# A weight product moved to the front of TensorE, with the first attention batch placed by hand inside it

## The chip, the cores and the metric

One core of one Trainium2 chip. The metric is the device time of one execution in microseconds (us), median of several executions; the profile's "span" of an execution is 1.7 to 2.3 us shorter in the runs of this case. Where a granted clock is given, it is the mean over an execution or a stretch of the clock that the profile says TensorE was granted (1.000 is full). "Half clock" below names a pace, read from the distance of matmuls of 512 columns: 0.42 to 0.43 us where the fastest stretches have 0.216 (kernel before, from 26.38 and from 29.74 us), or from other work that takes longer in such stretches (score groups 0.66 us instead of 0.43). The granted clock doesn't show every one of them (it reads 1.00 in that one); that the clock is the cause there is the author's reading.

## The reference

```python
scores = q @ k.T / 8                      # 8 batches, 8 heads, 576 positions, 64 channels
# heads 0-3 see the last 32 positions; heads 4-7 every 4th of the last 128
attn = softmax(where(mask, scores, -1e9))
x = (attn @ v) -> [4608, 512]             # heads side by side
a, b = x @ w1, x @ w2                     # 512 -> 1024
y = ((a * b) @ w3) @ w_out                # 1024 -> 1024 -> 512
```

Both kernels form `wf = w3 @ w_out` once on the chip, so that y is `(a * b) @ wf`: 64 matmuls in place of a whole layer.

## The kernel before

Four kinds of work share TensorE. The attention of a batch is four *steps* (dilated heads `d0`, `d1`, plain heads `p0`, `p1`), each of two score groups (12 small matmuls, exponential on ScalarE, mask on VectorE), values (12 matmuls, then reciprocal and scaling on VectorE) and a transpose to channels (6 matmuls and a copy into `XT`). `ffn1(t, f)` makes an eighth of a and b for block `t` (512 tokens) in 8 matmuls of 512 columns, and VectorE multiplies a by b. `ffn2(t, tb)` makes 128 rows of y in 8. The weight product has `fuse_t` (8 transposes of w3 and a copy to `w3T`) and `fuse_m` (8 matmuls and a copy to `wf`).

The attention is a list of *phases*. `point()` stands before each group of four large matmuls, and a table of marks (point number, phases done by then) says how many phases to place there:

```python
def fuse_t(ft):
    xv = ps_x.rearrange("p (g x) -> p g x", g=KFF)      # the bank that to_channels uses too
    for g in range(KFF):
        nc.tensor.transpose(out=xv[:, g, :], in_=w3n[ft // 2][...], identity=ident)
    w3T[ft] = wk_pool.tile([P, KFF, P], BF16, tag="w3T", bufs=2, name="w3T")
    nc.scalar.copy(out=w3T[ft], in_=xv)
...
load_qk(0, split=True); load_vp(0); load_w12(0, 512); load_qk(1); load_vd(1); load_vp(1)
load_w12(512, 1024); load_wo()
for g in range(4): load_w3(g)
for ph in phases[:n0]: ph()                  # batch 0, all its 22 phases
marks = [(0, n0), (9, n0), (30, done_at[7]), (32, done_at[7]), (54, done_at[11]), ...]
for f in range(KFF): ffn1(0, f, point)
fuse_t(0)
for ft in range(KFF):
    if ft + 1 < KFF: fuse_t(ft + 1)
    fuse_m(ft, point)
for f in range(KFF): ffn1(1, f, point)
for tb in range(4): ffn2(0, tb, point)
for t in range(2, NT): ...                   # two ffn1 of t, one ffn2 of t - 1, in turn
```

`done_at[7]` is the last phase of batch 1, `done_at[11]` of batch 2. Block 1 needs all of batch 1, block 2 all of batch 2, and so on.

The softmax here doesn't subtract the row's maximum and nothing guards it: scores larger than these inputs give would overflow.

Of the kernel before, what the change touches and what calls it, by code (L numbers as in the profile page):

```python
# [35 lines left out]
def kernel(  # L36
# [29 lines left out]
    stage = ExitStack()  # L66
    ps_early = stage.enter_context(tc.tile_pool(name="pse", bufs=1, space=bass.MemoryType.PSUM))
# [21 lines left out]
    ps_e = ps_early.tile([P, 2, TB], F32, name="ps_e")  # L89
    ffn_psum = []  # L90

    def bank():
        if not ffn_psum:
            ffn_psum.append(
                ctx.enter_context(
                    tc.tile_pool(name="psf", bufs=3, space=bass.MemoryType.PSUM)
                )
            )
        return ffn_psum[0].tile([P, TB], F32, tag="f", name="f")
# [4 lines left out]
    def load_qk(b, split=False):  # L104
        for nm, dst, src in (("qn", qn, q), ("kn", kn, k)):
            dst[b] = qk_pool.tile([P, 2, ROWS * D], BF16, tag=nm, name=nm)
        for u in (1, 0) if split else (slice(0, 2),):
            if split and u == 0:
                const_pool()
                load_vd(b)  # L110
            for dst, src in ((qn, q), (kn, k)):
                x = src[b].rearrange("(u h) (j a) d -> (h j) u (a d)", u=2, a=ROWS)
                nc.gpsimd.dma_start(out=dst[b][:, u], in_=x[:, u])  # L113
# [46 lines left out]
    def load_wo():  # L160
        nc.gpsimd.dma_start(out=wo_sb, in_=moe_w_out.rearrange("(a p) f -> p a f", p=P))
# [77 lines left out]
    class Step:  # L239
# [5 lines left out]
        def scores(self, hp, sp):  # L245
            u, hf = self.u, self.hf
            qt, kt = qts[u][self.b % 2], kts[u][self.b % 2]
            for m in range(3 * hf, 3 * hf + 3):
                for c in range(2):
                    for g in range(2):  # L250
                        prt = slice(32 * (2 * hp + g), 32 * (2 * hp + g) + 32)
                        if u:
                            rhs = qt[prt, 96 * m : 96 * m + 96, c]
                        else:
                            rhs = qt[prt].rearrange("p (s i) c -> p s i c", s=4)
                            rhs = rhs[:, :, 24 * m : 24 * m + 24, c]
                        c0 = 96 * (m - 3 * hf)
                        nc.tensor.matmul(  # L258
                            out=sp[:, g, c0 : c0 + 96],
                            lhsT=kt[prt, 96 * m : 96 * m + P, c],  # L260
                            rhs=rhs,
                            start=(c == 0),
                            stop=(c == 1),
                        )
# [3 lines left out]
            nc.scalar.activation(out=ev, in_=sp[:, :, 0:HALF], func=ACT.Exp, scale=scale)  # L268
# [62 lines left out]
    early = [True]  # L331
# [16 lines left out]
    def s_tile(hp):  # L348
        return ps_e if early[0] and hp else ps_s

    def later(f, *args):
        phases.append(lambda: f(*args))

    def segment(lo, hi):

        for i in range(lo, hi + 2):
# [5 lines left out]
            if i == lo:  # L362
                later(transpose_qk, b, 1, 0)
                later(transpose_qk, b, 1, 1)
                if lo:
                    later(spread_vd, b)
            if at == 2 and more:
                later(transpose_qk, b + 1, 1, 0)
            if at == 3 and more:
                later(transpose_qk, b + 1, 1, 1)  # L370
            if st is not None:
                later(lambda st=st: st.scores(0, s_tile(0)))
# [5 lines left out]
            if st is not None:  # L378
                later(lambda st=st: st.scores(1, s_tile(1)))
                if at == 0:  # L380
                    later(transpose_qk, b, 0, 0)
                    if b == 0:
                        later(spread_vd, 0)
                if at == 1:
                    later(transpose_qk, b, 0, 1)
                    later(prefetch, b + 2)
                if at == 3 and more:
                    later(spread_vd, b + 1)

    segment(0, 4)  # L390
# [42 lines left out]
    def ffn2(t, tb, point):  # L433
# [12 lines left out]
        o_sb = wk_pool.tile([P, d_model], F32, tag="osb", bufs=3, name="osb")  # L446
# [5 lines left out]
    def fuse_t(ft):  # L452
        xv = ps_x.rearrange("p (g x) -> p g x", g=KFF)
# [6 lines left out]
        w3T[ft] = wk_pool.tile([P, KFF, P], BF16, tag="w3T", bufs=2, name="w3T")  # L460
        nc.scalar.copy(out=w3T[ft], in_=xv)  # L461

    def fuse_m(ft, point):
        point()
        ps = bank()
        for g in range(KFF):
            if g == KFF // 2:
                point()
            nc.tensor.matmul(  # L469
                out=ps,  # L470
# [5 lines left out]
        nc.vector.tensor_copy(out=wf_sb[:, ft, :], in_=ps)  # L476
# [3 lines left out]
    load_qk(0, split=True)  # L480
    load_vp(0)
    load_w12(0, 512)
# [3 lines left out]
    load_w12(512, 1024)  # L486
    load_wo()
    for g in range(4):
        load_w3(g)

    const_spread()
    n0 = done_at[3]
    for ph in phases[:n0]:
        ph()
    early[0] = False
    stage.close()
# [4 lines left out]
        (0, n0), (9, n0), (30, done_at[7]), (32, done_at[7]), (54, done_at[11]),  # L501
    ]
    for t in range(3, 8):
        marks.append((54 + 24 * (t - 2), done_at[4 * t + 3]))
    xs, ys = [m[0] for m in marks], [m[1] for m in marks]
    state = [0, n0]
# [7 lines left out]

    for f in range(KFF):
        ffn1(0, f, point)
    fuse_t(0)
    for ft in range(KFF):
        if ft + 1 < KFF:
            fuse_t(ft + 1)  # L520
        fuse_m(ft, point)
    for f in range(KFF):
        ffn1(1, f, point)
    for tb in range(4):
        ffn2(0, tb, point)
    for t in range(2, NT):
# [37 lines left out]
```

## Time and profile before

| | before |
|---|---|
| time, median of 4 | 289.98 us (289.5 to 290.55) |
| first scores | 9.13 us |
| first a, b matmul | 26.38 us |
| first w3 transpose | 45.14 us |
| product of a and b for block 3, first of eight | 131.67 us |
| granted clock | 1.000 in the profiled run |

The rows are starting times in the trace. From block 3 on both kernels issue the same order of a, b and y, so the fourth row is where a gain or loss of the change must already be complete. The prediction shows the page and the busy time by stretches; the second and fourth row are these lines (start, duration, engine, line, operation; in brackets the idle time before and what ended it):

```profile
26.38 9.62 PE L406 MATMUL f<-XT,w_sb 128*128 128x512 bf16 x36 [0.73 <-ACT XT L327]
...
131.67 0.69 DVE L417 TENSOR_TENSOR gt<-f,asb 128x512 bf16<-128x512 f32 x1 [0.45 <-PE f L406]
```

### The profile page before, as it was taken

How to read it: one execution, taken by the hardware profiler on the slowest of the kernel's cores; microseconds unless marked ns; L12 is line 12 of the kernel's file. 1: busy time of each engine (PE TensorE's matmuls, PEld its weight loads, DVE VectorE, ACT ScalarE, POOL GpSimd, SP SyncE). 2: the span in 40 equal slices, each digit the busy share in tenths (PEclk: the TensorE clock that was granted, in tenths of full speed). 3: DMA queues.
4: the chain of work that ended last, by engine and by line, in shares of the span. 5: the costliest groups of instructions: out<-in, count | busy, mean ns of one | idle time of the engine just before them, and what ended most of it. 6: DMA issues, size and time to landing. Idle time of an engine off the chain costs nothing.

```text
span 288.0 us, 5662 instructions
## 1 busy us (share of the span) xinstructions
PE 260.3 (90%) x2336; PEld 131.8 (46%) x2336; DVE 164.8 (57%) x356; ACT 123.8 (43%) x200; POOL 53.7 (19%) x77
## 2 busy tenths in 40 slices
PE   0466988879899999999999999999999999999994
PEld 0353435444345545444444445445545544444441
DVE  5573385545798776767677767776764443222110
ACT  1543245543446455444544454455444433332422
POOL 8943512350042042006000600000000000000000
PEclk9999999999999999999999999999999999999999
DMA  7999999999069289567907991111111121111133
GB/s 102 156 207 190 198 211 210 202 194 144 0 102 171 75 166 173 80 116 130 137 36 124 145 147 42 39 36 39 39 36 39 36 56 55 36 73 36 48 85 126
DMA packets 50746, 30.51 MB, mean 106 GB/s; under 512 B 37920, under 2 KB 40992, under 8 KB 50720
## 3 DMA queue, kind: packets, MB, share of 16 engines
q0 software_dynamic: 45088, 20.71, 57.5%
q1 hardware_dynamic: 5632, 9.44, 10.9%
q8 instruction: 18, 0.29, 0.4%
q14 instruction: 8, 0.07, 0.1%
HBM read 41.41 MB, written 9.44 MB: 177 GB/s over the span
## 4 chain that ended last, share of the span: by engine, by line
PE 82%; DMA 9%; POOL 3%; ACT 2%; DVE 2%; issue 1%; POOLq 0%; ACTq 0%
PE f L406 41%; PE f L439 22%; PE ps_s L258 7%; DMA qn<-in_q_dram 5%; DMA w_sb<-in_moe_w_dram 4%; PE f L469 4%; PE ps_o L287 4%; PE ps_x L312 3%; PE ps_x L455 1%; ACT w3T L461 1%; POOL vst L137 1%; POOL vp L128 1%; POOL w_sb L155 1%; ACT et L268 0%; POOL qn L113 0%
## 5 line engine op out<-in xcount | busy, mean ns | idle before, releaser
L406 PE MATMUL f<-XT,w_sb 128*128 128x512 bf16 x576 | 138.8, 383 | 2.0 <-DMA w_sb<-in_moe_w_dram 1.3
L417 DVE TENSOR_TENSOR gt<-f,asb 128x512 bf16<-128x512 f32 x72 | 49.5, 687 | 55.5 <-PE f L406 55.3
L406 PEld LDWEIGHTS <-w_sb 128*128 128x128 bf16 x576 | 52.5, 98 | 61.1 <-issue 3.1
L439 PE MATMUL f<-wf_sb,gt 128*128 128x512 bf16 x288 | 70.8, 379 | 0.0
L416 ACT CAST asb<-f 128x512 bf16<-128x512 f32 x72 | 42.2, 586 | 54.3 <-PE f L406 49.6
L268 ACT ACTIVATE et<-ps_s 128x576 bf16<-128x576 f32 x60 | 39.2, 653 | 40.1 <-PE ps_s L258 39.9
L447 ACT COPY osb<-f 128x512 f32<-128x512 f32 x36 | 21.1, 586 | 45.7 <-PE f L439 45.7
L258 PE MATMUL ps_s<-qt,kt 32*128 32x96 bf16 x720 | 26.9, 206 | 13.8 <-DVE kt L230 10.1
L439 PEld LDWEIGHTS <-gt 128*128 128x128 bf16 x288 | 25.2, 98 | 25.2
L258 PEld LDWEIGHTS <-kt 32*128 32x128 bf16 x768 | 19.3, 97 | 37.0 <-issue 20.2
L297 DVE TENSOR_TENSOR xo<-ps_o,rcp 96x768 bf16<-96x768 f32 x32 | 30.5, 953 | 1.1
L137 POOL DMA_DIRECT2D vst<-in_v_dram x32 | 21.3, 672 | 13.9 <-DMA w3n<-in_moe_w_dram 4.4
L270 DVE TENSOR_TENSOR et<-et,mask_pl 128x576 bf16<-128x576 bf16 x32 | 14.6, 457 | 15.8 <-ACT et L268 15.5
L270 DVE TENSOR_TENSOR et<-et,mask_di 128x576 bf16<-128x576 bf16 x32 | 14.6, 456 | 14.7 <-ACT et L268 14.5
L230 DVE STREAM_TRANSPOSE qt<-qn 128x160 uint32<-128x160 uint32 (+1 forms) x64 | 19.6, 421 | 1.9 <-DMA qn<-in_q_dram 1.9
L287 PEld LDWEIGHTS <-et 128*128 128x128 bf16 x384 | 17.0, 102 | 7.7 <-issue 1.2
L312 PE MATMUL ps_x<-ident,xo 96*128 96x96 bf16 x192 | 14.4, 215 | 5.4 <-ACT w3T L461 2.3
L312 PEld LDWEIGHTS <-xo 96*128 96x128 bf16 x192 | 11.9, 102 | 12.5 <-DVE xo L297 4.1
L113 POOL DMA_DIRECT2D qn<-in_q_dram x9 | 6.3, 696 | 61.1 <-DVE qt L230 57.9
L296 DVE RECIPROCAL rcp<-ps_o 96x12 f32<-96x12 f32 x32 | 7.2, 225 | 16.4 <-PE ps_o L287 16.3
L469 PE MATMUL f<-wo_sb,w3T 128*128 128x512 bf16 x64 | 16.0, 380 | 0.0
L327 ACT COPY XT<-ps_x 128x576 bf16<-128x576 bf16 x18 | 11.5, 640 | 7.7 <-PE ps_x L312 7.7
(43 smaller groups left out, 113.8 us busy)
## 6 DMA issues: line engine op xcount, KB each, us to landing
qn<-in_q_dram POOLq DMA_DIRECT2D x7, 576.0 KB, 8.7
kn<-in_k_dram POOLq DMA_DIRECT2D x7, 576.0 KB, 7.8
vp<-in_v_dram POOLq DMA_DIRECT2D x7, 384.0 KB, 9.8
w_sb<-in_moe_w_dram POOLq DMA_DIRECT2D x4, 512.0 KB, 11.9
w3n<-in_moe_w_dram POOLq DMA_DIRECT2D x4, 512.0 KB, 18.7
out_dram<-osb SPq DMA_DIRECT2D x8, 256.0 KB, 2.3
out_dram<-osb SPq DMA_DIRECT2D x8, 224.0 KB, 2.3
out_dram<-osb SPq DMA_DIRECT2D x8, 192.0 KB, 2.2
```

Source lines behind the costliest of these rows:

```text
L137: nc.gpsimd.dma_start(out=vsts[b % 2][p0 : p0 + n, m, :, :], in_=bass.AP(tensor=x.tensor, offset=x.offset + (4 * i0 + 2 * second) * D, ap= ...
L258: nc.tensor.matmul(out=sp[:, g, c0 : c0 + 96], lhsT=kt[prt, 96 * m : 96 * m + P, c], rhs=rhs, start=(c == 0), stop=(c == 1),)
L268: nc.scalar.activation(out=ev, in_=sp[:, :, 0:HALF], func=ACT.Exp, scale=scale)
L270: nc.vector.tensor_tensor(out=ev, in0=ev, in1=mk.unsqueeze(1).to_broadcast([P, 2, HALF]), op=AL.mult)
L287: nc.tensor.matmul(out=ps_o[:, hp, j * (D + 1) : (j + 1) * (D + 1)], lhsT=self.et[:, c0 : c0 + P], rhs=rhs, start=True, stop=True,)
L297: nc.vector.tensor_tensor(out=xo[0:96], in0=ov[:, :, :, 0:D], in1=rcp[0:96].unsqueeze(3).to_broadcast([96, 2, 6, D]), op=AL.mult,)
L312: nc.tensor.transpose(out=xo, in_=self.xo[0:96, hp, 2 * m : 2 * m + 2, :], identity=ident[0:96, 0:96],)
L406: nc.tensor.matmul(out=ps, lhsT=w_sb[:, c, f * P : (f + 1) * P], rhs=XT[:, c, t0 + lo : t0 + hi], start=(c == 0), stop=(c == DCH - 1),)
L416: nc.scalar.copy(out=a_sb[:, 0 : hi - lo], in_=ps)
L417: nc.vector.tensor_tensor(out=gts[t][:, f, lo:hi], in0=pss[1], in1=a_sb[:, 0 : hi - lo], op=AL.mult)
L439: nc.tensor.matmul(out=y, lhsT=gts[t][:, f, tb * P : (tb + 1) * P], rhs=wf_sb[:, f, :], start=(f == 0), stop=(f == KFF - 1),)
L469: nc.tensor.matmul(out=ps, lhsT=w3T[ft][:, g, :], rhs=wo_sb[:, g, :], start=(g == 0), stop=(g == KFF - 1),)
```

## The change

The intent: TensorE's front is thin because it waits for the chain of attention steps of batch 0 (busy 9.4 of the first 26.3 us). The weight product doesn't depend on attention, so it could fill those waits. w3 and w_out are loaded first; the order in the front is written out by hand ("T": `fuse_t`, "M": half a `fuse_m`, "A": one attention phase); the w3T transposes leave the attention's bank and are copied by ScalarE and VectorE in turn; the second score buffer of the early stage goes; y of blocks 0 and 1 comes right behind their a and b, so that 24 points still pass before batch 1 must be done (its phases stand in the last 11 of them).

```diff
+    ps_f = ctx.enter_context(tc.tile_pool(name="psf", bufs=3, space=bass.MemoryType.PSUM))
-    ps_e = ps_early.tile([P, 2, TB], F32, name="ps_e")
...
-        xv = ps_x.rearrange("p (g x) -> p g x", g=KFF)
+        xv = bank().bitcast(BF16).rearrange("p (g x) -> p g x", g=KFF)
...
-        nc.scalar.copy(out=w3T[ft], in_=xv)
+        (nc.vector.tensor_copy if ft % 2 else nc.scalar.copy)(out=w3T[ft], in_=xv)
...
-    load_qk(0, split=True)
+    load_w3(0); load_wo(0); load_wo(1); const_pool(); load_w3(1); load_qk(0, 1)
+    load_w3(2); load_vd(0); load_qk(0, 0); load_w3(3)
     load_vp(0)
-    load_w12(0, 512)
+    load_w12(0, 256); load_w12(256, 1024)
...
+    for what in (
+        "T0 T1 M0 M0 M1 M1 T2 T3 M2 M2 M3 A M3 A T4 T5 M4 A M4 A M5 A M5 A "
+        "T6 T7 M6 A M6 A A M7 A A M7 A A A A A"
+    ).split(): ...
...
-        (0, n0), (9, n0), (30, done_at[7]), (32, done_at[7]), (54, done_at[11]),
+        (0, done_at[3]), (13, done_at[3]), (24, done_at[7]), (27, done_at[7]),
+        (47, done_at[11]), (53, done_at[11]), (64, done_at[15]),
...
+    for t in range(2):
+        for f in range(KFF): ffn1(t, f, point)
+        for tb in range(4): ffn2(t, tb, point)
     for f in range(KFF):
-        ffn1(0, f, point)
-    fuse_t(0)
-    ...
-    for t in range(2, NT):
+        ffn1(2, f, point)
+    for t in range(3, NT):
```

The 16 phases of batch 0 are, in order: four score groups of d0 and d1, values d0, values d1, channels d0, channels d1, four score groups of p0 and p1, values p0, values p1, channels p0, channels p1. Transposes of q and k and the copy of v (`spread_vd`) ride along with the phase that first needs them. In the kernel before they were phases of their own (hence 22 for batch 0), and the steps of batch 0 overlapped: the next step's scores stood before a step's values. Not shown in the cut: `w3T` gets three buffers in place of two and the tile of y six in place of three.

More of the change, by code (lines that the diff above doesn't have):

```diff
@@ L65 @@
     psum = ctx.enter_context(tc.tile_pool(name="ps", bufs=1, space=bass.MemoryType.PSUM))
-    stage = ExitStack()
-    ps_early = stage.enter_context(tc.tile_pool(name="pse", bufs=1, space=bass.MemoryType.PSUM))
+    ps_f = ctx.enter_context(tc.tile_pool(name="psf", bufs=3, space=bass.MemoryType.PSUM))
     w1_sb = const.tile([P, DCH, d_ff], BF16, name="w1_sb")
@@ L88, with load_qk @@
     ps_x = psum.tile([P, 2 * TB], BF16, name="ps_x")
-    ps_e = ps_early.tile([P, 2, TB], F32, name="ps_e")
-    ffn_psum = []
     def bank():
-        if not ffn_psum:
-            ffn_psum.append(
-                ctx.enter_context(
-                    tc.tile_pool(name="psf", bufs=3, space=bass.MemoryType.PSUM)
-                )
-            )
-        return ffn_psum[0].tile([P, TB], F32, tag="f", name="f")
+        return ps_f.tile([P, TB], F32, tag="f", name="f")
     qn, kn = {}, {}
-    def load_qk(b, split=False):
+    def load_qk(b, us=slice(0, 2)):
         for nm, dst, src in (("qn", qn, q), ("kn", kn, k)):
-            dst[b] = qk_pool.tile([P, 2, ROWS * D], BF16, tag=nm, name=nm)
-        for u in (1, 0) if split else (slice(0, 2),):
-            if split and u == 0:
-                const_pool()
-                load_vd(b)
-            for dst, src in ((qn, q), (kn, k)):
-                x = src[b].rearrange("(u h) (j a) d -> (h j) u (a d)", u=2, a=ROWS)
-                nc.gpsimd.dma_start(out=dst[b][:, u], in_=x[:, u])
+            if b not in dst:
+                dst[b] = qk_pool.tile([P, 2, ROWS * D], BF16, tag=nm, name=nm)
+            x = src[b].rearrange("(u h) (j a) d -> (h j) u (a d)", u=2, a=ROWS)
+            nc.gpsimd.dma_start(out=dst[b][:, us], in_=x[:, us])
     def load_vp(b):
@@ L158, in load_w12, with load_wo @@
             )
-    def load_wo():
-        nc.gpsimd.dma_start(out=wo_sb, in_=moe_w_out.rearrange("(a p) f -> p a f", p=P))
+    def load_wo(half):
+        a = slice(4 * half, 4 * half + 4)
+        nc.gpsimd.dma_start(
+            out=wo_sb[:, a, :], in_=moe_w_out.rearrange("(a p) f -> p a f", p=P)[:, a, :]
+        )
     w3n = {}
@@ L243, in __init__, with scores @@
             self.xo = {}
-        def scores(self, hp, sp):
+        def scores(self, hp):
             u, hf = self.u, self.hf
@@ L258, in scores @@
                         nc.tensor.matmul(
-                            out=sp[:, g, c0 : c0 + 96],
+                            out=ps_s[:, g, c0 : c0 + 96],
                             lhsT=kt[prt, 96 * m : 96 * m + P, c],
@@ L267, in scores @@
             )
-            nc.scalar.activation(out=ev, in_=sp[:, :, 0:HALF], func=ACT.Exp, scale=scale)
+            nc.scalar.activation(out=ev, in_=ps_s[:, :, 0:HALF], func=ACT.Exp, scale=scale)
             mk = (mask_di if u else mask_pl[:, hf]).rearrange("p m x -> p (m x)")
@@ L327, in to_channels @@
                 nc.scalar.copy(out=dst, in_=xv)
-    early = [True]
     steps = [
@@ L346, in prefetch, with along @@
             load_vp(b)
-    def s_tile(hp):
-        return ps_e if early[0] and hp else ps_s
+    ahead = []
+    def along(f, *args):
+        ahead.append(lambda: f(*args))
     def later(f, *args):
-        phases.append(lambda: f(*args))
+        todo = ahead + [lambda: f(*args)]
+        phases.append(lambda: [g() for g in todo])
+        ahead.clear()
     def segment(lo, hi):
@@ L364, in segment @@
                 later(transpose_qk, b, 1, 1)
-                if lo:
-                    later(spread_vd, b)
             if at == 2 and more:
-                later(transpose_qk, b + 1, 1, 0)
+                along(transpose_qk, b + 1, 1, 0)
             if at == 3 and more:
-                later(transpose_qk, b + 1, 1, 1)
+                along(transpose_qk, b + 1, 1, 1)
             if st is not None:
-                later(lambda st=st: st.scores(0, s_tile(0)))
+                if at == 1:
+                    along(transpose_qk, b, 0, 1)
+                later(st.scores, 0)
             if p2 is not None:
@@ L378, in segment, with first_batch @@
             if st is not None:
-                later(lambda st=st: st.scores(1, s_tile(1)))
                 if at == 0:
-                    later(transpose_qk, b, 0, 0)
-                    if b == 0:
-                        later(spread_vd, 0)
+                    along(transpose_qk, b, 0, 0)
+                    if i == lo:
+                        along(spread_vd, b)
+                later(st.scores, 1)
                 if at == 1:
-                    later(transpose_qk, b, 0, 1)
-                    later(prefetch, b + 2)
+                    along(prefetch, b + 2)
                 if at == 3 and more:
-                    later(spread_vd, b + 1)
-    segment(0, 4)
+                    along(spread_vd, b + 1)
+    def first_batch():
+        d0, d1, p0, p1 = steps[0:4]
+        along(transpose_qk, 0, 1, 0)
+        along(transpose_qk, 0, 1, 1)
+        for st in (d0, d1):
+            for hp in range(2):
+                later(st.scores, hp)
+        along(spread_vd, 0)
+        later(d0.values)
+        later(d1.values)
+        along(transpose_qk, 0, 0, 0)
+        along(transpose_qk, 0, 0, 1)
+        along(prefetch, 2)
+        later(d0.to_channels)
+        later(d1.to_channels)
+        for st in (p0, p1):
+            for hp in range(2):
+                later(st.scores, hp)
+        for st in (p0, p1):
+            later(st.values)
+        for st in (p0, p1):
+            later(st.to_channels)
+        done_at[3] = len(phases)
+    first_batch()
     segment(4, 8)
@@ L445, in ffn2 @@
             )
-        o_sb = wk_pool.tile([P, d_model], F32, tag="osb", bufs=3, name="osb")
+        o_sb = wk_pool.tile([P, d_model], F32, tag="osb", bufs=6, name="osb")
         nc.scalar.copy(out=o_sb, in_=y)
@@ L459, in fuse_t, with fuse_m @@
             )
-        w3T[ft] = wk_pool.tile([P, KFF, P], BF16, tag="w3T", bufs=2, name="w3T")
-        nc.scalar.copy(out=w3T[ft], in_=xv)
-    def fuse_m(ft, point):
-        point()
-        ps = bank()
-        for g in range(KFF):
-            if g == KFF // 2:
-                point()
+        w3T[ft] = wk_pool.tile([P, KFF, P], BF16, tag="w3T", bufs=3, name="w3T")
+        (nc.vector.tensor_copy if ft % 2 else nc.scalar.copy)(out=w3T[ft], in_=xv)
+    wf_ps = {}
+    def fuse_m(ft, half):
+        if half == 0:
+            wf_ps[ft] = bank()
+        for g in range(4 * half, 4 * half + 4):
             nc.tensor.matmul(
-                out=ps,
+                out=wf_ps[ft],
                 lhsT=w3T[ft][:, g, :],
@@ L475, in fuse_m @@
             )
-        nc.vector.tensor_copy(out=wf_sb[:, ft, :], in_=ps)
+        if half:
+            nc.vector.tensor_copy(out=wf_sb[:, ft, :], in_=wf_ps[ft])
     const_vector()
-    load_qk(0, split=True)
+    load_w3(0)
+    load_wo(0)
+    load_wo(1)
+    const_pool()
+    load_w3(1)
+    load_qk(0, 1)
+    load_w3(2)
+    load_vd(0)
+    load_qk(0, 0)
+    load_w3(3)
     load_vp(0)
-    load_w12(0, 512)
+    load_w12(0, 256)
+    load_w12(256, 1024)
     load_qk(1)
@@ L485 @@
     load_vp(1)
-    load_w12(512, 1024)
-    load_wo()
-    for g in range(4):
-        load_w3(g)
     const_spread()
-    n0 = done_at[3]
-    for ph in phases[:n0]:
-        ph()
-    early[0] = False
-    stage.close()
+    state = [0, 0]
+    for what in (
+        "T0 T1 M0 M0 M1 M1 T2 T3 M2 M2 M3 A M3 A T4 T5 M4 A M4 A M5 A M5 A "
+        "T6 T7 M6 A M6 A A M7 A A M7 A A A A A"
+    ).split():
+        if what == "A":
+            phases[state[1]]()
+            state[1] += 1
+        elif what[0] == "T":
+            fuse_t(int(what[1]))
+        else:
+            ft = int(what[1])
+            fuse_m(ft, int(ft in wf_ps))
+    assert state[1] == done_at[3]
     marks = [
-        (0, n0), (9, n0), (30, done_at[7]), (32, done_at[7]), (54, done_at[11]),
-    ]
-    for t in range(3, 8):
-        marks.append((54 + 24 * (t - 2), done_at[4 * t + 3]))
+        (0, done_at[3]), (13, done_at[3]), (24, done_at[7]), (27, done_at[7]),
+        (47, done_at[11]), (53, done_at[11]), (64, done_at[15]),
+    ]
+    for t in range(4, 8):
+        marks.append((63 + 24 * (t - 3), done_at[4 * t + 3]))
     xs, ys = [m[0] for m in marks], [m[1] for m in marks]
-    state = [0, n0]
     def point():
@@ L513, in point @@
             state[1] += 1
-    for f in range(KFF):
-        ffn1(0, f, point)
-    fuse_t(0)
-    for ft in range(KFF):
-        if ft + 1 < KFF:
-            fuse_t(ft + 1)
-        fuse_m(ft, point)
-    for f in range(KFF):
-        ffn1(1, f, point)
-    for tb in range(4):
-        ffn2(0, tb, point)
-    for t in range(2, NT):
+    for t in range(2):
+        for f in range(KFF):
+            ffn1(t, f, point)
+        for tb in range(4):
+            ffn2(t, tb, point)
+    for f in range(KFF):
+        ffn1(2, f, point)
+    for t in range(3, NT):
         for i in range(4):
```

## The prediction

> **What bounds the kernel now.** I read the page first, then busy time by stretches, then the chain of work that ended last, then the first 75 us instruction by instruction.
>
> ```profile
> span 288.0 us, 5662 instructions
> ...
> PE   0466988879899999999999999999999999999994
> ...
> DMA  7999999999069289567907991111111121111133
> GB/s 102 156 207 190 198 211 210 202 194 144 0 102 171 75 166 173 80 116 130 137 36 124 145 147 42 39 36 39 39 36 39 36 56 55 36 73 36 48 85 126
> ```
>
> The PE row is full from about 90 us to the end, and thin in the first quarter, where the DMA row is full: loading runs at about 200 GB/s until 70 us. So whatever the change can win lies before 75 us. The stretches put sizes on it (span, then busy PE, weight loads, DVE, ACT, POOL):
>
> ```profile
> 0.00:9.10 9.10, 0.00 (x0) 0.00 (x0) 4.64 (x31) 1.28 (x1) 7.72 (x19) 1.00 0.79 104
> 9.10:26.40 17.30, 9.47 (x169) 7.80 (x170) 10.66 (x22) 8.74 (x13) 9.38 (x12) 1.00 1.37 194
> 26.40:44.90 18.50, 17.18 (x111) 7.47 (x111) 10.12 (x25) 6.54 (x11) 6.43 (x9) 1.00 1.42 200
> 44.90:70.00 25.10, 20.76 (x240) 12.45 (x239) 12.44 (x22) 12.34 (x15) 8.25 (x10) 1.00 1.45 196
> 70.00:90.00 20.00, 18.96 (x188) 9.15 (x186) 17.06 (x42) 9.18 (x16) 5.47 (x7) 1.00 0.58 77
> 90.00:130.00 40.00, 40.00 (x415) 20.41 (x414) 28.52 (x62) 18.92 (x33) 6.19 (x8) 1.00 0.88 124
> ```
>
> TensorE waits 9.1 us for the first q and k, then does the attention of batch 0 alone for 17.3 us; from 26.4 us it works on a, b and the weight product, idle 1.3 us (a load of w1, w2) and 4.3 us (the weight product). The chain shows what dense work costs; it has one piece for each wait or run of matmuls:
>
> ```profile
> 25.19 12.07 DMA w_sb<-in_moe_w_dram
> 37.31 1.90 PE f L406 x8
> ...
> 52.84 1.02 ACT w3T L461
> 53.90 0.41 PE ps_x L312 x6
> ...
> 75.56 0.97 PE f L406 x4
> 76.53 0.37 PE ps_s L258 x9
> 76.89 0.97 PE f L406 x4
> ...
> 275.28 8.65 PE f L439 x40
> ```
>
> Forty matmuls of 512 columns take 8.65 us: 0.216 us each. From 75.1 us to the last matmul at 283.9 us the kernel does 792 of them (504 of a, b and 288 of y), 171 us, and six batches of attention; (208.8 - 171) / 6 = 6.3 us of TensorE for a batch. With these the old time closes: start of a, b 26.4; 864 matmuls 186.5; weight product 64 x 0.216 + 8 transpose groups x 0.46 = 17.5; seven batches 44.1; slow clock at the start of a, b 1.7; stalls 7.8 (1.3, about 5.5 in the weight product with its drains, 1.0 where batch 2 starts); tail after the last matmul 4.05. Sum 288.05 against 288.0.
>
> [...] the first a, b matmuls at 26.38 us come 0.42 us apart and are at 0.216 from 29.74, 3.4 us later, although the page's clock row shows nines. Hence the 1.7 us above. [...] scores complete at 11.19 us had their exponential only at 12.27, behind the 1.47 us copy of v that ScalarE had begun at 10.91. [...]
>
> **The change part by part.** It removes no arithmetic. It moves the weight product (17.5 us) in front of a, b, interleaved with the attention of batch 0; loads w3 and w_out first; spreads the w3T copies over two engines; drops the second early score buffer, so that scores of one step wait for each other's exponential; and does y of blocks 0 and 1 directly behind their a, b.
>
> Loads. At 512 KB in 2.5 us (w3 before) and with a first landing near 6.5 us (q's half-size load took 4.2 us from 1.3), I estimate landings of w3 part 0 6.5, w_out 9 and 11.7, w3 part 1 14.3, k of the dilated heads 17, w3 part 2 19.7, v 22, the other q, k 25, w3 part 3 27.5, w1/w2 first quarter 32.5, the rest 40, batch 1 complete at 50.
>
> TensorE's front, with durations of the trace. The second pair of w3T transposes can run at 14.4 at best, perhaps 16 if the first product is at slow clock; plus 1.0 for the ScalarE copy: the third product starts at about 16.3 (m). The transposes of q and k are queued on VectorE behind the copy of that product: 1.73 (8 matmuls) + 0.75 (copy) + 2.4 (eight transposes) puts the first scores at m + 4.9, with TensorE idle 2.3. Four score groups, three half products, the next two transposes with 1.0 of copy behind an exponential, bring the fourth scores to m + 10.9. The v copy of batch 0 still sits on ScalarE behind the exponential (0.65 + 1.5), so values of step 0 come at m + 13.2; reciprocal and scaling (1.2) hold step 1 to m + 15. The last w3T transposes and copy end at m + 17. Six passes of halves, channels and scores, with 2.5 of VectorE transposes and one exponential exposed, put the last scores at m + 23.7. Behind them: score and exponential 1.15, mask 0.5, scaling of the step before 1.25, values 0.55, reciprocal and scaling 1.25, transpose to channels 0.45, copy 0.7: 5.9 us in which TensorE does nearly nothing. a, b start at m + 29.6 = 45.9 us, 19.5 later than before, for 17.5 us of work brought forward.
>
> Stalls behind. Batch 1 gets its 18 phases within 11 insertion points (before: 21). VectorE needs about 14.7 us for a batch (transposes 4.9, eight masks 3.7, four reciprocal-and-scaling 4.7, copies 1.4) plus 0.69 for each a x b, while TensorE passes 11 points and a batch in 9.5 + 6.3 = 15.8 us. My walk gives 4 to 5 us of waits: 1.6 for first transposes, two exponentials of 0.75, 1.5 behind VectorE, 0.5 at the end. I take 4.0. Batch 2 starts as before, 1.0. Batch 3 is again squeezed into 11 points, beside six a x b: VectorE 18.2 against TensorE 15.8, so at least 2.1.
>
> Sum: 45.9 + clock 1.2 (it may stay fast in part) + 186.5 + 44.1 + stalls 7.1 + tail 4.05 = 288.9 us of span. The old run took 289.68 by the clock for a span of 288.0; adding 1.7 gives 290.5.
>
> **The rivals.** First, the intent holds: the front is bound by loads alone. If the last w3 part at 27.5 were the only gate, a, b would start near 40.4 and stalls of 5 would give 281 of span, some 283 us, over 2% faster. For it speaks that TensorE's first quarter is so empty and that someone placed each phase by hand; against it, the queue order on VectorE and ScalarE, which no landing time alters. Second, clock and squeeze combine badly: with TensorE idle a third of the front it may stay at half clock, as it did from 9 to 26 us before; the later products then cost up to 5 more, and the two squeezed batches up to 10: about 298. Against it: the old weight-product stage idled about a sixth and stayed fast. Third, loads become the bound after the front, as for the old 1.3 us wait: if w1, w2 landed later than 47 they would gate a, b; my estimate of 40 leaves slack, so this adds nothing.
>
> **Range and chances.** Sum of a front uncertain by 2 and stalls uncertain by 3, with a longer side toward fast because the hand placement was probably tried on a chip: 284 to 296. Over 2% faster means under 284.0, over 2% slower above 295.6. I give 0.15 faster, 0.72 within, 0.13 slower.
>
> **What would show it.** Right: a first a, b matmul at 44.5 to 47.5 us; first scores some 4.9 us after the third product starts, released by VectorE's k transpose; step-0 values released by ScalarE's v copy; 5 to 6 us between the last early scores and the first a, b; VectorE at nine tenths or more in the two squeezed batches with TensorE idle there. Wrong: a, b starting by 41, waits named for DMA rather than VectorE inside the front, or a full PE row behind it; then the time is near 283.

45.9 + 1.2 + 186.5 + 44.1 + 7.1 + 4.05 comes to 288.9 us of span and 290.5 by the clock. The two terms for slow matmuls, 1.7 before and 1.2 after, rest on the trace alone (0.42 us apart from 26.38 us, 0.216 from 29.74). The landings estimated under "Loads" come from 512 KB in 2.5 us in the kernel before. Two readings of the kernel before lack their numbers in the text: "half clock from 9 to 26 us" are score groups of 0.66 us from 10.53 on against 0.43 from 39.14 on (the clock row reads nines in both), and "stayed fast" is the weight product with a clock of 1.00 and four matmuls in 1.02 to 1.04 us. The 5 and 10 us that the second rival adds are estimates, without a derivation.

## The result, and the profile after

| | before | after | predicted after |
|---|---|---|---|
| time, median of 4 | 289.98 us (289.5 to 290.55) | 294.28 us (293.82 to 295.42) | 290.5 (284 to 296) |
| first scores | 9.13 us | 24.22 us | 21.2 |
| first a, b matmul | 26.38 us | 49.68 us | 45.9 |
| block 3's first a x b | 131.67 us | 137.42 us | |
| span of the profiled run | 288.0 us | 293.5 us | 288.9 |
| granted clock of the executions | 1.000 (profiled) | 0.983 to 0.988 | |

The ratio of the times is 1.0153, 95% interval 1.0115 to 1.0192. The change costs 1.5%, which is inside 2% either way, and in the two profiled executions the loss is complete at block 3: 5.75 us there and 5.5 at the end. The profiled execution of the changed kernel is the slowest of its four (295.42 us with a span of 293.5 and a clock of 0.983; the others have spans of 291.8 to 292.7 and 0.988), so what follows shows somewhat more loss than the medians, which differ by 4.3 us.

The page of the changed kernel:

```profile
span 293.5 us, 5618 instructions
...
PE   0797774979879999988999999999999999999994
...
PEclk9997998997999999999999999999999999999999
```

The first four slices of the PE row are fuller than before (0797 against 0466; over the first ten the sums are 66 and 65), yet the run is longer: some of that busyness is matmuls at half clock. A part of it is visible as sevens and eights in the clock row, which was all nines before; the twelve slow matmuls at 12.50 us below (0.43 us apart) are not: the granted clock from 6.5 to 20 us reads 1.00. Busy time is not progress.

The front instruction by instruction. Columns are start, duration, engine, line, operation, output and inputs, shapes, how many; in brackets the idle time before and what ended it:

```profile
9.51 1.86 PE L486 MATMUL f<-wo_sb,w3T 128*128 128x512 bf16 x4 [0.94 <-DMA wo_sb<-in_moe_w_out_dram]
12.50 5.28 PE L486 MATMUL f<-wo_sb,w3T 128*128 128x512 bf16 x12 [1.13 <-DMA wo_sb<-in_moe_w_out_dram]
17.58 1.38 PE L472 MATMUL f<-ident,w3n 128*128 128x128 bf16 x16
19.62 2.76 PE L486 MATMUL f<-wo_sb,w3T 128*128 128x512 bf16 x11 [0.66 <-ACT w3T L478]
21.55 0.69 DVE L494 CAST wf_sb<-f 128x512 bf16<-128x512 f32 x1 [1.80 <-PE f L486]
22.16 1.20 DVE L219 STREAM_TRANSPOSE qt<-qn 128x160 uint32<-128x160 uint32 x4
23.21 1.19 DVE L219 STREAM_TRANSPOSE kt<-kn 128x160 uint32<-128x160 uint32 x4
24.22 0.43 PE L247 MATMUL ps_s<-qt,kt 32*128 32x96 bf16 x12 [1.84 <-DVE kt L219]
...
32.03 1.46 ACT L134 COPY vd<-vst 128x1536 bf16<-128x1536 bf16 x1
33.55 0.52 PE L276 MATMUL ps_o<-vd,et 128*128 128x65 bf16 x12 [1.13 <-ACT vd L134]
...
43.89 0.44 PE L247 MATMUL ps_s<-qt,kt 32*128 32x96 bf16 x12
...
46.69 0.52 PE L276 MATMUL ps_o<-vp,et 128*128 128x65 bf16 x12 [1.89 <-DVE xo L286]
...
48.53 0.43 PE L301 MATMUL ps_x<-ident,xo 96*128 96x96 bf16 x6 [1.06 <-DVE xo L286]
...
49.68 0.58 PE L423 MATMUL f<-XT,w_sb 128*128 128x512 bf16 x1 [0.73 <-ACT XT L316]
```

Twelve matmuls take 5.28 us at 12.50 us, and the next twelve (eleven records) 2.76 at 19.62 us: half clock, then full. (From 24.6 to 28.5 us TensorE is at half clock once more: four matmuls take 1.45 us and sixteen transposes 1.89, against 1.04 and 1.05 later, with a granted clock of 0.66 from 24 to 29 us.) How long the twelve take is partly luck. Nine kernels of the experiments issue the same matmuls up to the third product, without fillers, and there the twelve took 2.75 to 5.28 us and the third product began at 16.87 to 20.33 us. Three of them leave the whole front as it is (batch 1 spread out, no hold, old order of y); they start a, b at 47.51, 50.29 and 47.54 us. So differences of up to 3 us in the start of a, b need more than one pair of traces; a safer measure is the time from the third product on.

Before the third product TensorE waits for loads (0.94 and 1.13 us for the halves of w_out). From it (19.62) on, every wait is the one that the prediction walked through: transposes of q and k queued behind the copy of the third product although k's load had landed at 17.8 us; the v copy on ScalarE; and 5.8 us between the last early scores (43.89) and the first a, b (49.68).

Behind the front, batch 1 squeezed into 11 points:

```profile
64.31 0.43 PE L247 MATMUL ps_s<-qt,kt 32*128 32x96 bf16 x12 [1.07 <-DVE kt L219]
...
65.49 0.43 PE L247 MATMUL ps_s<-qt,kt 32*128 32x96 bf16 x12 [0.74 <-ACT et L257]
...
65.86 1.75 PE L423 MATMUL f<-XT,w_sb 128*128 128x512 bf16 x4
...
67.54 0.66 PE L247 MATMUL ps_s<-qt,kt 32*128 32x96 bf16 x12
...
68.13 1.67 PE L423 MATMUL f<-XT,w_sb 128*128 128x512 bf16 x4
```

A wait for k's transposes, one for an exponential (two score groups with no other work between them), and then TensorE is at half clock again: four matmuls in 1.75 us where they take 1.04 at full clock. The waits alone don't decide this: the kernel with the v copy on VectorE (below) has the same two waits there, 1.08 and 0.74 us, and its next four matmuls, at 63.87 us, take 1.04.

And busy time in the two squeezed stretches (span, then busy PE, weight loads, DVE, ACT, POOL, clock, DMA share, GB/s):

```profile
62.00:82.80 20.80, 17.37 (x211) 9.23 (x214) 15.30 (x35) 9.20 (x15) 5.49 (x7) 0.92 0.94 130
...
117.00:134.80 17.80, 15.67 (x216) 8.88 (x216) 16.24 (x38) 9.43 (x16) 1.14 (x2) 1.00 0.76 81
```

In the second (batch 3) VectorE is busy 91%, and TensorE waits 1.0 us for VectorE's `XT` copy and 0.9 for an exponential. In the first (batch 1) VectorE is busy 74% only: there it is single waits (1.5 us for exponentials, 1.1 for k's transposes, 0.5 for a scaling), not VectorE's throughput.

The balance of the profiled runs, with the prediction's 186.5 us for 864 matmuls and 44.1 us for seven batches (230.6 together):

| term, us | before | after | predicted after |
|---|---|---|---|
| start of a, b | 26.4 | 49.7 | 45.9 |
| large matmuls and batches 1 to 7 | 230.6 | 230.6 | 230.6 |
| weight product behind the start | 17.5 | 0 | 0 |
| stalls and half clock behind the start (the remainder) | 9.5 | 9.2 | 8.3 |
| tail after the last matmul | 4.05 | 4.0 | 4.05 |

17.5 us of work went out from behind the start of a, b, and the start moved 23.3 us. The difference of 5.8 us is the loss of the profiled execution; the remaining terms nearly cancel. From block 3 on nothing is added:

```profile
137.42 0.68 DVE L434 TENSOR_TENSOR gt<-f,asb 128x512 bf16<-128x512 f32 x1
```

### The profile page after: what moved, and what is told of

The parts are those of the page before. It is cut to its first block, busy times and chain, and to the rows that moved or that the text cites. A ratio compares the mean times of both kernels' runs of the same rounds, so it can differ in the third digit from the quotient of the medians.

```text
span 293.5 us, 5618 instructions
## 1 busy us (share of the span) xinstructions
PE 261.9 (89%) x2294; PEld 131.8 (45%) x2336; DVE 165.0 (56%) x360; ACT 120.2 (41%) x196; POOL 54.4 (19%) x78
## 4 chain that ended last, share of the span: by engine, by line
PE 82%; DVE 8%; DMA 3%; ACT 3%; issue 2%; POOL 1%; ACTq 0%; DVEq 0%; POOLq 0%
PE f L423 42%; PE f L456 21%; PE ps_s L247 8%; PE f L486 4%; PE ps_o L276 4%; DMA wo_sb<-in_moe_w_out_dram 3%; PE ps_x L301 3%; DVE xo L286 2%; DVE qt L219 2%; ACT et L257 1%; DVE kt L219 1%; ACT w3T L478 1%; DVE gt L434 1%; PE f L472 1%; DVE kt L212 1%
## 5 line engine op out<-in xcount | busy, mean ns | idle before, releaser
L423 PEld LDWEIGHTS <-w_sb 128*128 128x128 bf16 x576 | 51.8, 98 | 58.6 <-issue 4.7
L456 PE MATMUL f<-wf_sb,gt 128*128 128x512 bf16 x274 | 69.1, 379 | 1.1 <-issue 0.5
L257 ACT ACTIVATE et<-ps_s 128x576 bf16<-128x576 f32 x64 | 41.7, 652 | 36.4 <-PE ps_s L247 36.4
L456 PEld LDWEIGHTS <-gt 128*128 128x128 bf16 x288 | 25.9, 98 | 26.9
L247 PE MATMUL ps_s<-qt,kt 32*128 32x96 bf16 x768 | 28.3, 204 | 7.2 <-DVE kt L219 4.0
L486 PE MATMUL f<-wo_sb,w3T 128*128 128x512 bf16 x60 | 19.3, 454 | 3.8 <-DMA wo_sb<-in_moe_w_out_dram 2.1
L276 PEld LDWEIGHTS <-et 128*128 128x128 bf16 x384 | 15.7, 98 | 10.5 <-issue 4.1
L301 PEld LDWEIGHTS <-xo 96*128 96x128 bf16 x192 | 11.3, 97 | 8.7 <-DVE xo L286 2.1
L301 PE MATMUL ps_x<-ident,xo 96*128 96x96 bf16 x192 | 13.5, 206 | 1.5 <-DVE xo L286 1.5
```

The source lines that it names most:

```text
L247: nc.tensor.matmul(out=ps_s[:, g, c0 : c0 + 96], lhsT=kt[prt, 96 * m : 96 * m + P, c], rhs=rhs, start=(c == 0), stop=(c == 1),)
L257: nc.scalar.activation(out=ev, in_=ps_s[:, :, 0:HALF], func=ACT.Exp, scale=scale)
L276: nc.tensor.matmul(out=ps_o[:, hp, j * (D + 1) : (j + 1) * (D + 1)], lhsT=self.et[:, c0 : c0 + P], rhs=rhs, start=True, stop=True,)
L301: nc.tensor.transpose(out=xo, in_=self.xo[0:96, hp, 2 * m : 2 * m + 2, :], identity=ident[0:96, 0:96],)
L423: nc.tensor.matmul(out=ps, lhsT=w_sb[:, c, f * P : (f + 1) * P], rhs=XT[:, c, t0 + lo : t0 + hi], start=(c == 0), stop=(c == DCH - 1),)
L456: nc.tensor.matmul(out=y, lhsT=gts[t][:, f, tb * P : (tb + 1) * P], rhs=wf_sb[:, f, :], start=(f == 0), stop=(f == KFF - 1),)
```

## The experiments

Three theories for the front. A: the order of the queues on VectorE and ScalarE sets it, and the squeezed batches cost stalls behind it. B: the loads set it. C: the granted clock sets what A leaves over. All kernels gave correct results. Times below are medians of the runs of each, with 294.28 us for the changed kernel, which was run only in its own rounds, and 289.75 to 290.17 us for the kernel before, which was run again in the rounds of each experiment. Every ratio is to the kernel before of the same rounds (the changed kernel: 1.0153, 1.0115 to 1.0192). Times of the changed kernel and its variants scatter by 1.4 to 4 us, those of the kernel before by 1.7 at most; so what an edit does in its own place is read from the trace, and the total is quoted beside it.

**First transposes earlier in VectorE's queue.**

```diff
-        "T0 T1 M0 M0 M1 M1 T2 T3 M2 M2 M3 A ...
+        "T0 T1 M0 M0 M1 M1 T2 T3 Q M2 M2 M3 A ...     # Q: transposes of q, k that rode with the first A
```

> Only the place of the first eight q and k transposes in VectorE's queue changes: ahead of the third product's copy instead of behind it. Theory A (queue order on VectorE and ScalarE bounds the front): k of the dilated heads landed at 17.8 us, so the first scores come at about 22.4 instead of 24.2 us, a, b start 1.8 us earlier (47.9 instead of 49.7), total 292.5 instead of 294.3. Theory B (loads bound the front): a, b start and total unchanged.

Measured: 292.75 us (292.06 to 293.42), ratio to before 1.0103 (1.0078 to 1.0129). From the trace of this run:

```profile
17.51 1.06 PE L470 MATMUL f<-ident,w3n 128*128 128x128 bf16 x16
19.22 2.76 PE L484 MATMUL f<-wo_sb,w3T 128*128 128x512 bf16 x11 [0.66 <-ACT w3T L476]
19.28 1.22 DVE L219 STREAM_TRANSPOSE qt<-qn 128x160 uint32<-128x160 uint32 x4
20.34 1.21 DVE L219 STREAM_TRANSPOSE kt<-kn 128x160 uint32<-128x160 uint32 x4
21.41 0.67 DVE L492 CAST wf_sb<-f 128x512 bf16<-128x512 f32 x1
21.92 0.44 PE L247 MATMUL ps_s<-qt,kt 32*128 32x96 bf16 x12
```

The transposes now stand ahead of the product's copy, and the first scores follow the start of the third product by 2.7 us instead of 4.6, with no wait. From there to a, b (46.56 us) it takes 27.3 us in all, against 29.0 and 29.3 in two kernels with the unchanged front that stayed at full clock from 24 to 28 us (sixteen transposes in 1.07 us there): 1.7 to 1.9 us won, 1.8 expected. No load changed. A holds here, B doesn't. (That a, b start 3.1 us before the changed kernel's 49.68 is in part a luckier clock.)

**The v copy of batch 0 on VectorE.**

```diff
-        copy = nc.vector.tensor_copy if b else nc.scalar.copy
+        copy = nc.vector.tensor_copy
```

> The v copy of batch 0 goes to VectorE (0.55 us) instead of ScalarE (1.47 us behind an exponential). Theory A: the values of step 0 start near 32.7 instead of 33.55 us and a, b about 0.9 us earlier, total near 293.4. Theory B: unchanged, v landed at 22.2 us.

Measured: 294.22 us (292.5 to 295.37), ratio 1.0168 (1.0129 to 1.0206). In its place the edit did half of what A says: the copy takes 0.55 us instead of 1.46, but TensorE's wait before the values of d0 shrinks only from 1.13 to 0.74 us. (The values start 6.2 us after the third pair of w3 transposes instead of 7.0, but in the changed kernel those transposes ran at half clock (1.89 us instead of 1.07); where they ran at full clock with the copy still on ScalarE it was 6.6.) The total doesn't show it: its four executions differ by 2.9 us. Inconclusive for the time.

**Batch 1 spread over all 24 points.**

```diff
-        (0, done_at[3]), (13, done_at[3]), (24, done_at[7]), (27, done_at[7]),
+        (0, done_at[3]), (24, done_at[7]), (27, done_at[7]),
```

> Batch 1's phases are spread over the 24 points from the start of a, b on, instead of the last 11 of them. Theory A (the squeeze costs stalls of 4 to 5 us between 62 and 83 us): block 1's a, b starts 3 us earlier than 82.8, total near 291.3, and the half-clock matmuls at 65.9 and 68.1 us are gone. Theory B (batch 1's loads hold it back): its v of the plain heads landed at 51.3 and k at 46.9, so an early start would wait for loads and gain under 0.5 us.

Measured: 290.37 us (289.9 to 292.74), ratio 1.0038 (0.9994 to 1.0082). Block 1's first a x b comes 32.3 us after the start of a, b instead of 35.1: 2.8 us won in its place, against an estimate of 3. (This profiled run also had a luckier front, 47.5 us.) Luck of the front doesn't enter this measure: in six other kernels with the squeeze it is 35.2 to 36.1 us. From the start of a, b to the end of the span this run takes 241.1 us; the six kernels that keep both squeezes take 243.8 to 244.8. It is the largest gain of a single edit here, and the loads of batch 1 did not stand in the way. The half clock at 65.9 and 68.1 us is gone, as A says: from 58 us on the clock row of this run is all nines (0.92 from 62 to 82.8 us in the changed kernel), and four matmuls take 1.02 to 1.04 us. But so it is in the kernel with the v copy on VectorE, which keeps the squeeze (nines from 51 us on, 1.04 us at 63.87 and 65.20).

**No hold before batch 3.**

```diff
-        (47, done_at[11]), (53, done_at[11]), (64, done_at[15]),
+        (47, done_at[11]), (64, done_at[15]),
```

> Batch 3's phases are spread over 17 points instead of 11 (the hold between points 47 and 53 goes). Theory A (VectorE has 18 us of work for 16 of TensorE there): block 3's first a x b product ends 2 us earlier than 137.4, total near 292.3. Rival: VectorE catches up later anyway and the stall only moves, total unchanged within 0.5.

Measured: 293.48 us (292.09 to 294.79), ratio 1.0128 (1.0084 to 1.0172). In the traces block 3's first a x b follows block 1's by 50.6 us instead of 52.7, the 2 us expected; the medians differ by 0.8 with overlapping intervals, so the total doesn't settle it. The trace speaks against the rival that the stall only moves: from the start of a, b to the end of the span this run takes 242.0 us, against 243.8 to 244.8 where both squeezes stay.

**The last quarter of w3 loaded later.**

```diff
-    load_w3(3)
     load_vp(0)
     load_w12(0, 256)
+    load_w3(3)
```

> The last quarter of w3 is loaded behind v of the plain heads and the first quarter of w1, w2, so it lands about 5 us later (near 32.5 instead of 27.5 us). Theory A (engine order bounds the front): its transposes start at 35.7 us anyway, so a, b start and total stay as in the changed kernel within 0.7 us (that is the spread of its runs). Theory B (loads bound the front): both move by up to 5 us, total near 299.

Measured: 295.17 us (293.63 to 297.07), ratio 1.0178 (1.0122 to 1.0235), against 1.0153 for the changed kernel. The transposes of that quarter start at 35.91 us (35.74 in the changed kernel) and a, b at 50.09 (49.68). This quarter landed at 33.8 us instead of 27.5, and the front moved by 0.4 us, less than it differs between runs of one front. So this load doesn't set it, and B falls for the part from the third product on. The total is 0.9 us higher, more than the 0.7 of A, with overlapping intervals: not resolved. No run moved the loads before the third product, w_out and the first half of w3, and there TensorE does wait for them.

**TensorE's early waits filled with matmuls that nothing needs.**

```diff
-        "T0 T1 M0 M0 M1 M1 T2 ...
+        "D8 T0 T1 D8 M0 D12 M0 M1 M1 T2 ...           # Dn: n matmuls of 128 columns on the identity
```

> 28 extra matmuls of 128 columns on the identity, into a bank that nothing reads before it is overwritten, fill TensorE's waits between 5.2 and 12.5 us. Theory C (the clock that TensorE is granted is what my estimate of the front missed): the twelve matmuls that took 5.28 us from 12.50 us take 2.6, the second pair of w3 transposes starts near 15.1 instead of 17.6 us, a, b about 2.5 us earlier, total near 291.8. If the clock is not the cause: no change, or the extra matmuls' time on top.

Measured: 293.3 us (291.72 to 294.13), ratio 1.0098 (1.0057 to 1.0139). The same twelve matmuls as in the changed kernel:

```profile
13.11 2.75 PE L486 MATMUL f<-wo_sb,w3T 128*128 128x512 bf16 x12 [1.76 <-DMA wo_sb<-in_moe_w_out_dram]
...
15.70 1.06 PE L472 MATMUL f<-ident,w3n 128*128 128x128 bf16 x16
```

2.75 us instead of 5.28: the same matmuls at full clock. That the fillers did it is not shown by this trace alone, for the next kernel has none and the same order up to there, and its twelve took as little:

```profile
12.57 2.75 PE L486 MATMUL f<-wo_sb,w3T 128*128 128x512 bf16 x12 [1.57 <-DMA wo_sb<-in_moe_w_out_dram]
```

Of ten profiles without fillers this one alone has 2.75 us; both with fillers have it. So it is likely that they help. a, b start at 47.41 us, 2.3 us earlier than in the changed kernel's profile but only 0.1 earlier than in two of the unfilled kernels with its front (47.51, 47.54). The total is about 1 us lower with overlapping intervals, and the granted clock (0.979 to 0.988) no higher than in the changed kernel: in this trace the pace drops again later in the front (four matmuls in 1.47 us at 26.00) and in batch 1 (1.89 at 65.88). A gain in time is not shown.

**Product first, attention after it, nothing interleaved.**

```diff
+        "T0 T1 M0 M0 M1 M1 T2 T3 M2 M2 M3 M3 T4 T5 M4 M4 M5 M5 "
+        "T6 T7 M6 M6 M7 M7 A A A A A A A A A A A A A A A A"
```

> The whole weight product first, then the sixteen phases of batch 0's attention in one piece. If the placing by hand inside the product pays, as the change intends: a, b start near 54.5 instead of 49.7 us and the total is near 299. Rival: the phases only wait for the same copies and exponentials elsewhere, a, b start within 1 us of 49.7.

Measured: 306.87 us (306.01 to 307.74), ratio 1.0579 (1.0544 to 1.0614); a, b start at 60.82. So the interleaving is worth some 11 us at the start of a, b (10.5 to 13.3 with the spread of that start), over twice the 4.8 that I expected. PE and clock rows of this run:

```profile
PE   1785534498998999998899999999999999999994
...
PEclk9999955579799999999999999999999999999999
```

During the attention alone, from 38 to 61 us, TensorE is three to four tenths busy and is granted five tenths of its clock (the mean over the executions is 0.948 to 0.955); its score groups take 0.66 us there instead of 0.43. I had counted the waits but no half clock. This is the clearest view of theory C.

**The old order of y behind the new front.**

```diff
-    for t in range(2):  # ffn1(t), then ffn2(t)
+    # ffn1(0), ffn1(1), ffn2(0), then the old loop from t = 2
-        (0, n0), (13, n0), (24, d7), (27, d7), (47, d11), (53, d11), (64, d15)    # d7: done_at[7]
+        (0, n0), (16, d7), (38, d11), (63, d15)
```

> The front of the change with the old order behind it (a, b of block 1 right behind block 0, then y of block 0, then the old loop), so batch 1 has 16 points from the start of a, b on, batch 2 22 and batch 3 25. Theory A: against the run in which batch 1 started at once with 24 points (290.4 us) it loses 1 to 2 us to VectorE in batch 1 and wins 2 in batch 3: 290 to 292. If y behind its own a, b is worth something by itself: over 293.

Measured: 290.05 us (288.74 to 292.72), ratio 1.0010 (0.9947 to 1.0074), the same as the run with batch 1 spread over 24 points (1.0038). Two things changed at once, the place of y and the marks, and the expected costs and gains of the marks offset each other. Moving y costs or wins nothing that these runs resolve. Against the changed kernel both runs agree that batches spread over more points are faster.

**One part of the change alone, in the kernel before.**

```diff
 # in the kernel before, nothing else changed
-        xv = ps_x.rearrange("p (g x) -> p g x", g=KFF)
+        xv = bank().bitcast(BF16).rearrange("p (g x) -> p g x", g=KFF)
-        w3T[ft] = ... bufs=2 ...;  nc.scalar.copy(out=w3T[ft], in_=xv)
+        w3T[ft] = ... bufs=3 ...;  (nc.vector.tensor_copy if ft % 2 else nc.scalar.copy)(out=w3T[ft], in_=xv)
```

> One part of the change alone, in the kernel before: the w3T transposes go to one of the three rotating banks and are copied by ScalarE and VectorE in turn, instead of all through the one bank that the attention also uses. TensorE idled 4.3 us in that stage, over 2 us of it between w3T copies and the attention's transposes to channels. If that bank is the cause: 1.5 to 2.5 us less, 287.5 to 288.5. If not: 290 as before.

Measured: 286.47 us (285.9 to 286.7), ratio 0.9880 (0.9863 to 0.9898), granted clock 0.998 to 1.000. Busy time in the weight product's stretch, to be held against the same stretch of before in the prediction (20.76 us of PE):

```profile
44.90:70.00 25.10, 23.30 (x249) 13.60 (x251) 16.87 (x32) 8.87 (x12) 7.89 (x10) 1.00 1.45 196
```

TensorE idles 1.8 us there instead of 4.3, and block 1's first a x b comes 4.0 us earlier (71.62 instead of 75.60). I had counted only the waits that name the shared bank (1.5 to 2.5 us). The edit does three things, own bank, second copy engine and a third buffer of `w3T`; which of them wins how much is not separated. This small part of the change, left where the product was, beats the kernel before. The rest of the change, the move with its queue order and marks, turned a gain of 3.5 us into a loss of 4.3.

**All found waits mended.** The transposes and the v copy earlier (both on VectorE), the last w3 transposes before the values of d0, values of p0 before the last score group, batch 1 over 24 points, no hold:

```diff
+        "T0 T1 M0 M0 M1 M1 T2 T3 Q M2 M2 M3 A M3 A T4 T5 M4 A V M4 A T6 T7 M5 A M5 A "
+        "M6 A M6 A A M7 A A A M7 A A A A"                # V: the v copy of batch 0
+        (0, done_at[3]), (24, done_at[7]), (27, done_at[7]), (47, done_at[11]), (64, done_at[15]),
```

> The change with its found waits mended together: first q, k transposes and v copy earlier in VectorE's queue, last w3 transposes before the values of step 0, values of the first plain step before the last scores, batch 1 from the first point on, no hold before batch 3. Theory A: a, b start near 45.5 instead of 49.7 us, 1.5 (first scores) + 1.5 (last w3 copy and tail) + 3.6 (batch 1) + 0.7 (batch 3) off 294.3: 287, about 1% under the kernel before. If the gains do not add because loads bind then: 289 to 290.

Measured: 287.5 us (285.28 to 288.12), ratio 0.9911 (0.9880 to 0.9942). a, b start at 46.01 us, 26.8 us after the third product instead of 30.1, and 239.1 us before the end of the span instead of 243.8. The interval lies clear of the changed kernel's (1.0115 to 1.0192). The sum of the parts came out near the 287 expected and below the 289 to 290 of the rival, which is the best evidence for A.

**The mended kernel with filled waits.**

```diff
+        "D8 T0 T1 D8 M0 D16 M0 M1 M1 T2 ... M7 A D10 A D10 A D10 A D6"
```

> The mended kernel with 68 extra matmuls of 128 columns on the identity in TensorE's waits before 12.5 us and between the last scores and the first a, b. Theory C (clock): the first products and the first a, b matmuls run at full clock, 2 to 3 us less than the mended kernel, near 284.5. If the clock is not the cause: equal or slower by the extra matmuls' 4 us.

Measured: 285.41 us (284.63 to 287.49), ratio 0.9860 (0.9828 to 0.9891). Its six executions sort by clock: the two at 1.000 took 284.63 and 284.70 us, the two at 0.979 and 0.982 took 287.49 and 287.10. None of the mended kernel's six reached 1.000 (0.973 to 0.991). The median is 2.1 us lower, as expected, but the intervals of the two ratios just overlap. Its profiled run, one of the slow pair, shows where the clock was lost:

```profile
25.41 0.44 PE L247 MATMUL ps_s<-qt,kt 32*128 32x96 bf16 x12
28.31 1.89 PE L470 MATMUL f<-ident,w3n 128*128 128x128 bf16 x16 [2.47 <-DMA w3n<-in_moe_w_dram]
29.99 1.91 PE L484 MATMUL f<-wo_sb,w3T 128*128 128x512 bf16 x4
```

With the waits before the first scores and before the values of d0 gone (1.84 and 1.13 us in the changed kernel), and these transposes placed earlier in the order, TensorE reaches the last quarter of w3 before its load does (2.47 us; 0.94 in the mended kernel without fillers), and comes back at half clock (sixteen transposes in 1.89 us instead of 1.07, four matmuls in 1.91 instead of 1.04). So beyond the third product a load does bind, but only once the queue order is mended: the first rival of the prediction was the next limit, not the present one.

**The mended front with the old order of y.**

> The mended front with the old order of y behind it. The two orders gave 290.4 and 290.1 on the unmended front, so 287 again within 1; if y behind its own a, b helps once the front is short: over 288.5.

Measured: 288.34 us (287.34 to 288.79), ratio 0.9941 (0.9920 to 0.9961), 0.8 us above the mended kernel with intervals that overlap. Not resolved; here too the marks changed with the order.

## Why the prediction was right, and where it was off

- **Mechanism of the front: right.** From the third product's start (m) to the first a, b I had m + 29.6; the trace has 30.06. First scores m + 4.6 (I said 4.9), released by VectorE's transposes; last early scores to a, b 5.8 (said 5.9). The runs with earlier transposes (27.3 us instead of 29.0 to 30.1) and with a later load of w3 (0.4 us) show that these are queue waits and not that load.
- **Size of m: off by 3.3 us.** I put the third product at 16.3 us; it began at 19.62. Two things in it: w_out's second half landed at 12.5 instead of 11.7, and both first products ran at half clock (twelve matmuls in 5.28 us), of which I had allowed for only a part. In other profiles the same twelve took as little as 2.75 us, so part of the 3.3 is luck of this execution; the ten unfilled profiles put m at 16.87 to 20.33, all above my 16.3. This is the mis-sized term of the sum: a, b start at 49.7 instead of 45.9, 3.8 of the 4.6 us by which the profiled span (293.5) exceeds the forecast (288.9). It also put the start outside my own sign of 44.5 to 47.5 us, and one of my signs of being wrong showed in part: two waits inside the front are named for DMA, both before m.
- **Stalls behind: right in sum, 9.2 against 8.3, which is partly luck.** Batch 1's squeeze was confirmed by spreading it out (2.8 us in its place), batch 3's by dropping the hold (2 us in its place). Of the sign that I named, VectorE at nine tenths in both, only batch 3 shows it (91%); batch 1 (74%) lost its time to single waits and then to half clock at 65.9 and 68.1 us, which my sum did not contain. The two squeezes gave back 2.8 and 2.0 us where I had put 4.0 and 2.1; the other 4.4 us, beside my 2.2 for clock and batch 2, are half clock and smaller waits that no run separates.
- **The chances were right, the centre was 3.8 us low.** I gave 0.72 for a result within 2%; it is 1.5% slower, 1.3 us short of what I called over 2% slower. I had lengthened the range toward fast because the hand placement looked tried. That was no evidence.
- **Rivals.** Loads as the only bound: refuted for the changed kernel from the third product on, and found as the next bound in the mended one. That the loads had no rate to spare was not shown: the kernel before shows 194 to 200 GB/s from 9.1 to 70 us and nines in the DMA row from 7 to 72 us, and no run shows a ceiling. (A small slip: 864 x 0.216 is 186.6, not 186.5; it stands in every column and cancels.) Clock and squeeze together at their worst, 298: half true, the granted clock did drop (0.66 from 24 to 29 us, 0.92 from 62 to 82.8), but the time came to 294.3. w1, w2 as the bound behind the front: not seen, the first a, b waited for the last `XT` copy (0.73 us).

What stays open: which pattern of waits makes the clock drop. The kernel before, with waits of 1.10, 1.16 and 1.16 us in its weight product, kept full clock (1.00); the changed kernel lost it at 65.9 us (four matmuls in 1.75 us, 1.04 at full clock) after a 1.07 and a 0.74 us wait, and the kernel with the v copy on VectorE kept it after the same two. The kernel without interleaving was at full clock after a wait of 2.98 us (28.82 us), the mended one with fillers at half after 2.47. From 38 to 61 us the kernel without interleaving was granted five tenths with no wait over 2.1 us. No run isolates the rule, and since the clock differs between executions, each clock reading here is one draw.

## What to carry to other kernels

Filling an engine's waits with independent work paid here, against 290.0 us before, only once the other engines' queues and the marks behind it were mended (294.3 us, then 287.5): until then the early work waited on VectorE and ScalarE behind what stood ahead in their queues (1.84 us for k's transposes behind the third product's copy, 1.13 for the v copy behind an exponential). Judge such a move by when the following stage starts against how much work was taken from behind it (here 23.3 against 17.5 us), not by how full the row looks. Try the small parts of a large change on their own in the old kernel: here the second copy engine, the transposes' own bank and a third buffer gave 1.2% without the move. And compare several traces of one front before reading a difference of 2 us in it: here the start of a, b moved by 2.8 us between kernels with the same front.
